# Where the token factors, the weight shares and the conversion's first step stand inside a group of a two-layer MLP

## The chip, the core and the metric

The kernel runs on one core of one Trainium2 chip. The core has five instruction streams that wait for each other through semaphores: TensorE (PE; its weight loads, PEld, overlap its matmuls), VectorE (DVE), ScalarE (ACT), GpSimd (POOL) and SyncE (SP), which here only starts DMAs. Each stream runs its instructions in the order in which they were written into it. The metric is the device time of one execution in microseconds (us). The kernel before takes 1313.79 us, the median of three runs (1312.47 to 1313.97).

## The reference

```python
# x: (2, 3008, 256); attention-like mixing along the sequence
X = np.fft.rfft(x, axis=1); Xr, Xi = X.real, X.imag
Yr = Xr @ w_r - Xi @ w_i + b_r
Yi = Xr @ w_i + Xi @ w_r + b_i
Yr, Yi = (np.sign(v) * np.maximum(np.abs(v) - 0.01, 0.0) for v in (Yr, Yi))
t = np.fft.irfft(Yr + 1j * Yi, n=3008, axis=1).reshape(6016, 256)
# two MLP layers, w_in: (256, 2048), w_out: (2048, 256)
h = t @ w_in1;  t = (h / (1 + np.exp(-1.702 * h))) @ w_out1
h = t @ w_in2;  t = (h / (1 + np.exp(-h))) @ w_out2
```

The four MLP weights arrive as float64 bit patterns (int64 arrays), and the kernel turns them into fp32 itself. Every matrix operand is split into a rounded part ("hi", made by ACT) and the rest ("lo", a subtraction on DVE or POOL), and each product is three matmuls: hi by hi, hi by lo, lo by hi.

## The kernel before, in words

**Stages.** The first 224 us hold a forward transform as matmuls, the mixing with its threshold ("mid"), and the inverse transform. Then comes the MLP. Its 6016 tokens are cut into six blocks: five of 1024 tokens and a last one of 896. A block is handled as two halves of n columns (n is 512, in the last block 448). For each of the two layers and each block there are eight **groups** p = 0 to 7, one for each pair of 128-wide chunks of the 2048 hidden features: 96 groups in all, written (layer, block, p). The function `group` is one of them.

**A group.** The four hidden quarters (two chunks by two halves) come out of seven products rather than eight, with seven **token factors** x0 to x6 (sums and differences of quarters of the block) and seven weight factors. `prod(X, 5, 4)` adds the product of weight factor 5 and token factor x4 to PSUM bank X; it is three matmuls. PE's order in a group is: x0, x1, six output matmuls, x2, x3, twelve output matmuls, x4, x6, six output matmuls, x5. That makes 21 matmuls on L774 and 24 on L746, 45 in all. The output matmuls (`out_next`) use the activations of the group before. Around them ACT copies and DVE adds: y1 is a copy of X (L796) plus Y (L798); y2 a copy of Z (L806) plus the later X (L815); y3 a copy of the same X (L808) plus the later Z (L819); y4 is taken from X directly. Each y goes through the activation (L777), a cast to hi (L779) and a subtraction for lo (L784; three on POOL, one on DVE). As X and Z are summed up in steps, PE may go on only when a step has been read: x3 after the copy L796, x4 after the copy L808, x6 after L806, x5 after the add L815, and the next group's x2 after the activation of y4. The y values lie in the columns of `yt` that held the block's own tokens.

**A border.** The last group of a block (p = 7) and the first of the next (p = 0) prepare the next block's token factors in `xprep`: a cast on ACT (L99), a subtraction on DVE (L100), and for two of them another on DVE that turns the temporary `tmp` into the next factor (L697, L699). x0 to x3 belong to p = 7, x4 to x6 to p = 0. `xsums`, in p = 6, makes two sums ahead of them.

**Weights inside the MLP.** A 128-by-256 unit of float64 is loaded (`cv_load`), ACT takes an absolute value (L155), DVE does five steps (L160 to L164, kept in the list `fill` and let out by `pump` and `fills`), and `settle` adds the two parts (L223). Block (0, 0) converts two units in each group, blocks (0, 1) to (0, 4) one, and the rest none. Units of the second layer are written to DRAM. In the last block of layer 0 and the first groups of layer 1, `fetch` brings them back and `moved` splits them into PE's operands: `place_in` with sums, four casts on ACT and eight DVE steps, `place_out` with a cast and a subtraction each.

**What sets the order.** `hook(h)` is called at six places in a group, and says what else is written there. The MLP from the second group on stands in regions that are kept in written order on all engines; the stages before and the first group are put in order by a scheduler's cost model (PE in the inverse stage, POOL and SP in the forward stage and SP in the mid stage are kept in written order there too). At the start of a region its first instructions can move ahead of the last ones of the region before. Which engine gets some steps is read from the table CFG, one letter for each call in turn (V is DVE, P is POOL).

Of the kernel before, what the change touches and what calls it, by code (L numbers as in the profile page):

```python
# [1047 lines left out]
```

## Time and profile before

| what | value |
|---|---|
| median of the three runs | 1313.79 us |
| the profiled execution's own time / its span | 1313.38 us / 1311.6 us |
| busy in the span: PE, PEld, DVE, ACT, POOL | 1217.0, 975.3, 723.2, 801.5, 545.3 us |
| PE idle in front of L774 / of L746 | 60.5 us / 2.2 us |
| chain that ended last, by engine | PE 50%, DVE 20%, ACT 16%, issue 5% |
| first stages (to 224 us): PE, DVE busy | 194.5, 205.9 us |
| mean granted TensorE clock | 0.973 |

Busy time is the sum of an engine's instructions. A line of the timeline is: start in us, duration, engine, source line, operation, output<-inputs, how many instructions were merged (x6), and in brackets how long the engine had been idle and what ended that. The granted clock is a share of full speed (2.4 GHz); 0.5 is 1.2 GHz.

### The profile page before, as it was taken

The numbers are of one execution on the slowest core, as the hardware profiler recorded it, in microseconds if no ns is written. First come the engines' busy times: TensorE is split into PE (matmuls) and PEld (weight loads), VectorE is DVE, ScalarE is ACT, GpSimd is POOL, SyncE is SP. The second block draws the span as 40 slices with busy tenths as digits, with TensorE's granted clock in tenths as the row PEclk, the third lists the DMA queues.
The fourth block names the chain that finished last, engine by engine and source line by source line (L and its number), as shares of the span: only waits on it lengthen the run. The fifth ranks groups of instructions, "written<-read, shape, count | busy, mean of one in ns | idle before, by whom it ended". The sixth has DMA issues, their size and how long they took to land.

```text
span 1311.6 us, 15384 instructions
## 1 busy us (share of the span) xinstructions
PE 1217.0 (93%) x5220; PEld 975.3 (74%) x5220; DVE 723.2 (55%) x1266; ACT 801.5 (61%) x1585; POOL 545.3 (42%) x472
## 2 busy tenths in 40 slices
PE   7899888798899899998999988999999999999998
PEld 4777677576687687786787866877868868778797
DVE  7899999767656555555555464243342332433422
ACT  3566644566565666656666766666666665665665
POOL 4665654454343434443443333333333333333333
PEclk9889979889899999999999989999999999999999
DMA  8441131111111110111110110000000000000000
GB/s 314 171 141 52 58 138 47 33 49 32 44 41 32 32 43 28 38 36 36 33 36 8 34 48 17 1 1 33 0 32 1 0 33 0 1 33 0 33 1 29
DMA packets 33010, 57.09 MB, mean 44 GB/s; under 512 B 3233, under 2 KB 22689, under 8 KB 31650
## 3 DMA queue, kind: packets, MB, share of 16 engines
q1 hardware_dynamic: 30882, 41.42, 9.9%
q0 software_dynamic: 2048, 14.68, 3.1%
q8 instruction: 41, 0.67, 0.2%
q14 instruction: 39, 0.32, 0.1%
...
## 4 chain that ended last, share of the span: by engine, by line
PE 50%; DVE 20%; ACT 16%; issue 5%; POOL 0%; DVEq 0%; ACTq 0%
PE o L746 25%; PE x L774 22%; ACT yt L777 6%; ACT g L779 4%; DVE x L100 3%; PE psi L358 2%; DVE yt L815 2%; ACT x L99 2%; ACT yt L796 2%; DVE yt L798 1%; DVE cv_c L160 1%; DVE cv_c L164 1%; DVE cv_a L162 1%; DVE th L521 1%; DVE f L537 1%
## 5 line engine op out<-in xcount | busy, mean ns | idle before, releaser
L784 POOL TENSOR_TENSOR g<-yt,g 128x512 fp32r<-128x512 f32 (+1 forms) x288 | 367.0, 1287 | 649.5 <-PE x L774 289.0
L774 PE MATMUL x<-x,wi 128*128 128x512 f32 (+1 forms) x2016 | 530.3, 400 | 60.5 <-DVE yt L815 24.8
L746 PE MATMUL o<-g,wo 128*128 128x512 f32 (+1 forms) x2304 | 582.2, 395 | 2.2 <-POOL g L784 1.3
L746 PEld LDWEIGHTS o<-g,wo 128*128 128x128 f32 x2304 | 438.6, 191 | 101.2 <-POOL g L784 3.1
L774 PEld LDWEIGHTS x<-x,wi 128*128 128x128 f32 x2016 | 378.0, 191 | 170.2 <-DVE yt L815 27.6
L777 ACT ACTIVATE yt<-yt 128x512 f32<-128x512 f32 (+1 forms) x288 | 179.1, 622 | 346.6 <-DVE yt L815 252.4
L779 ACT CAST g<-yt 128x512 fp32r<-128x512 f32 (+1 forms) x384 | 234.2, 611 | 12.0
L798 DVE TENSOR_TENSOR yt<-yt,x 128x512 f32<-128x512 f32 (+1 forms) x96 | 64.9, 676 | 184.1 <-ACT yt L796 175.8
L815 DVE TENSOR_TENSOR yt<-yt,x 128x512 f32<-128x512 f32 (+1 forms) x96 | 64.6, 673 | 166.7 <-PE x L774 166.0
L784 DVE TENSOR_TENSOR g<-yt,g 128x512 fp32r<-128x512 f32 (+1 forms) x96 | 65.3, 681 | 63.5 <-ACT g L779 63.5
L100 DVE TENSOR_TENSOR x<-yt,x 128x512 fp32r<-128x512 f32 (+1 forms) x48 | 47.0, 980 | 59.9 <-ACT x L99 59.4
L160 DVE TENSOR_SCALAR cv_c<-cv_c 128x256 f32<-128x256 f32 x64 | 45.9, 718 | 44.0 <-ACT cv_c L155 44.0
L819 DVE TENSOR_TENSOR yt<-yt,x 128x512 f32<-128x512 f32 (+1 forms) x96 | 64.6, 673 | 0.6
L806 ACT COPY yt<-x 128x512 f32<-128x512 f32 (+1 forms) x96 | 54.5, 568 | 13.8 <-DVE x L100 13.8
L796 ACT COPY yt<-x 128x512 f32<-128x512 f32 (+1 forms) x96 | 54.9, 571 | 3.3 <-PE x L774 3.2
L777 ACT ACTIVATE yt<-x 128x512 f32<-128x512 f32 (+1 forms) x96 | 56.2, 585 | 0.2 <-PE x L774 0.2
L808 ACT COPY yt<-x 128x512 f32<-128x512 f32 (+1 forms) x96 | 55.7, 580 | 0.6 <-PE x L774 0.6
L358 PE MATMUL psi<-m,fh 128*128 128x376 f32 (+3 forms) x208 | 52.3, 341 | 0.2 <-DVE sd L511 0.2
L223 POOL TENSOR_TENSOR cv_a<-cv_a,cv_c 128x256 f32<-128x256 f32 x48 | 41.0, 857 | 9.9 <-DVE cv_c L164 9.9
L498 PE MATMUL psm<-wc_hi,xtl 128*128 128x512 f32 x96 | 38.0, 399 | 5.1 <-DVE xtl L100 5.1
L358 PE MATMUL psf<-m,xh 128*128 128x376 f32 (+1 forms) x160 | 39.5, 343 | 2.5 <-ACT xh L309 1.5
L358 PE MATMUL psi<-m,fl 128*128 128x376 f32 (+3 forms) x104 | 36.0, 346 | 6.2 <-POOL fl L100 3.3
(121 smaller groups left out, 1098.2 us busy)
## 6 DMA issues: line engine op xcount, KB each, us to landing
...
```

The costliest lines, as they stand in the source:

```text
L100: (lo_eng or nc.vector).tensor_sub(lo, src, r32(hi))
L160: lambda: ts(c, c, C_HI, None, op0=ALU.min),
L358: nc.tensor.matmul(ps, a, z, start=i == 0 and x == 0, stop=i == last and x == 2)
L746: nc.tensor.matmul(acc[h, mm], st, mv, start=first and k == 0, stop=last and k == 2)
L774: nc.tensor.matmul(ps, st, mv, start=first and m == 0, stop=m == 2, skip_group_check=True)
L777: nc.scalar.activation(g, g if src is None else src, func)
L779: nc.scalar.copy(gh, g)
L784: eng.tensor_sub(gl, g, r32(gh))
L796: nc.scalar.copy(y1, X)
L798: nc.vector.tensor_add(y1, y1, Y)
L815: nc.vector.tensor_add(y2, y2, X)
L819: nc.vector.tensor_add(y3, y3, Z)
```

## The change

Five things, all in the written order:

1. The token factors. `xprep` can be called in two parts (cast, subtraction). In p = 7, x0 goes from hook 2 to hook 1 (ahead of y1's activation), x1 and x2 from hook 3 to hook 2 (ahead of the copies of y2 and y3), x3's cast goes from hook 4 to hook 3 (ahead of y2's activation instead of behind it), and its subtraction stays at hook 4, which itself is moved behind the adds of y2 and y3. In p = 0, x4 goes to hook 1 and x6 to hook 2; x5 stays at hook 3. `xsums` goes to hook 1.
2. The absolute values (L155) go from hook 2 to hook 1, ahead of y1's activation; in blocks without conversions all fill steps are let out at once behind hook 2.
3. The fetched weights: `fetch` is written one group ahead, `place_in` goes from hook 3 to hook 2 and all its subtractions to DVE, `place_out`'s subtractions all go to POOL.
4. In CFG, `cva` goes from 'PPVP' to 'P' and `pil` from 'PPVV' to 'P': all L223 adds and all subtractions of freshly converted input weights go to POOL. The spare quarter of `yt` is no longer their temporary; `tmp` is.
5. The storage of y2 and y3 is exchanged, so that y2 overwrites the quarter that x1 and the last `tmp` step read, and y3 the one that x4 reads.

```diff
-    def xprep(l, i, k):
+    def xprep(l, i, k, part=3):
...
-        hi, lo = (slot(0, F32R, "x")[:, :n] for _ in range(2))
-        split(hi, lo, src, lo_eng=E('xl1' if l else 'xl0' if i == 0 else 'xl', k))
-        xb[l, i, k] = (hi, lo)
-        if k == 2:
-            nc.vector.tensor_sub(xtmp[0], b22, xtmp[0])
-        if k == 3:
-            nc.vector.tensor_sub(xtmp[0], b21, xtmp[0])
+        if part & 1:
+            xb[l, i, k] = tuple(slot(0, F32R, "x")[:, :n] for _ in range(2))
+            nc.scalar.copy(xb[l, i, k][0], src)
+        if part & 2:
+            hi, lo = xb[l, i, k]
+            E('xl1' if l else 'xl0' if i == 0 else 'xl', k).tensor_sub(lo, src, r32(hi))
+            if k in (2, 3):
+                nc.vector.tensor_sub(xtmp[0], b22 if k == 2 else b21, xtmp[0])
...
-        (y1, y2), (y3, y4) = y
-        spare[:] = [y4]
+        (y1, y3), (y2, y4) = y
...
-        fills(2)
+        fills(1 if l or i == last else 2)
...
-        hook(4)
         prod(Z, 6, 6, False)
         nc.vector.tensor_add(y3, y3, Z)
         rest(nc.vector, *g22)
         g12 = gate(0, 1, y3)
         rest(nc.gpsimd, *g12)
+        hook(4)
...
-                    place_in(l, c + r, a, E('mvl', r), sums_c)
+                    place_in(l, c + r, a, nc.vector, sums_c)
                 else:
-                    place_out(l, c + r, a, E('mvl', r))
+                    place_out(l, c + r, a, nc.gpsimd)
...
-            for x in {2: (0,), 3: (1, 2), 4: (3,)}.get(h, ()) if more else ():
-                xprep(*nxt, x)
-            for x in {2: (4,), 3: (6, 5)}.get(h, ()) if p == 0 else ():
-                xprep(l, i, x)
-            if h == 2 and p == NPR - 2 and (l, i) != (1, last):
+            if more:
+                if h in (1, 2):
+                    for x in ((0,), (1, 2))[h - 1]:
+                        xprep(*nxt, x)
+                if h == 3:
+                    xprep(*nxt, 3, 1)
+                if h == 4:
+                    xprep(*nxt, 3, 2)
+            if p == 0 and h < 4:
+                xprep(l, i, {1: 4, 2: 6, 3: 5}[h])
+            if h == 1 and p == NPR - 2 and (l, i) != (1, last):
                 xsums(*nxt)
-            if h == (3 if len(done) < 3 else 2):
+            if h == (3 if len(done) < 3 else 1):
                 window(0, done)
                 done[:] = []
-            if h == 2:
+            if h == 1:
                 window(k, ())
-            if h == 3:
-                moved(fetched)
+            if h in (2, 3):
+                moved([f for f in fetched if (f[0][0] == "in") == (h == 2)])
             if h == 5:
+                fetched[:] = fetch_for(at + 1)
+            if h == 4:
                 pump()
```

**Place 1, DVE at the border from block (0, 2) to (0, 3).** Before, from y1's add in p = 7 (L798) to the same add in the next group; L815 and L819 are the adds of y2 and y3, L784 an activation's lo, and x and tmp are the token factors and their temporary:

```order
L798 TENSOR_TENSOR yt<-yt,x 128x512
L100 TENSOR_TENSOR x<-yt,x 128x512
...
L100 TENSOR_TENSOR x<-yt,x 128x512
L100 TENSOR_TENSOR x<-tmp,x 128x512
L697 TENSOR_TENSOR tmp<-yt,tmp 128x512
L163 TENSOR_SCALAR cv_c<-cv_a 128x256
...
L815 TENSOR_TENSOR yt<-yt,x 128x512
L100 TENSOR_TENSOR x<-tmp,x 128x512
L699 TENSOR_TENSOR tmp<-yt,tmp 128x512
L819 TENSOR_TENSOR yt<-yt,x 128x512
L784 TENSOR_TENSOR g<-yt,g 128x512
L798 TENSOR_TENSOR yt<-yt,x 128x512
```

The same stretch of the changed kernel, where the four adds and the lo are L800, L817, L820, L800 and L786, and the token factors L699 and L701:

```order
L800 TENSOR_TENSOR yt<-yt,x 128x512
L699 TENSOR_TENSOR x<-yt,x 128x512 x2
L699 TENSOR_TENSOR x<-tmp,x 128x512
L701 TENSOR_TENSOR tmp<-yt,tmp 128x512
L160 TENSOR_SCALAR cv_c<-cv_c 128x256
...
L817 TENSOR_TENSOR yt<-yt,x 128x512
L820 TENSOR_TENSOR yt<-yt,x 128x512
L786 TENSOR_TENSOR g<-yt,g 128x512
L699 TENSOR_TENSOR x<-tmp,x 128x512
L701 TENSOR_TENSOR tmp<-yt,tmp 128x512
L800 TENSOR_TENSOR yt<-yt,x 128x512
```

x3's subtraction and the `tmp` step behind it have gone from between the adds of y2 and y3 to behind y2's lo; the fill steps have gone behind x0, x1 and x2.

**Place 2, ACT at the same border.** Before, from the copy of y1 in p = 7 to the activation of y2 (L777 the activations, L779 the casts to hi, L99 the casts of token factors, L155 the absolute value):

```order
L796 COPY yt<-x 128x512
L777 ACTIVATE yt<-yt 128x512
L779 CAST g<-yt 128x512
L99 CAST x<-yt 128x512
L155 ACTIVATE cv_c<-raw_4547 128x256
L806 COPY yt<-x 128x512
L808 COPY yt<-x 128x512
L99 CAST x<-yt 128x512
L99 CAST x<-tmp 128x512
L777 ACTIVATE yt<-yt 128x512
```

The same in the changed kernel (L798, L808 and L810 are the copies, L779 and L781 the activation and its cast, L696 the token factors):

```order
L798 COPY yt<-x 128x512
L696 CAST x<-yt 128x512
L155 ACTIVATE cv_c<-raw_4545 128x256
L779 ACTIVATE yt<-yt 128x512
L781 CAST g<-yt 128x512
L696 CAST x<-yt 128x512
L696 CAST x<-tmp 128x512
L808 COPY yt<-x 128x512
L810 COPY yt<-x 128x512
L696 CAST x<-tmp 128x512
L779 ACTIVATE yt<-yt 128x512
```

x0's cast and the absolute value now stand ahead of y1's activation, and the casts of x1 and x2 ahead of the copies of y2 and y3.

**Place 3, ACT in the second group of the last block of layer 0**, where input weights (wi) that were fetched (cv_ld) and their sums (cv_s) are split. Before:

```order
L779 CAST g<-yt 128x448
L806 COPY yt<-x 128x448
L808 COPY yt<-x 128x448
L99 CAST wi_6328<-cv_ld 128x256
L99 CAST wi_6328<-cv_ld 128x128
L99 CAST wi_6328<-cv_s 128x256 x2
L777 ACTIVATE yt<-yt 128x448
```

Changed:

```order
L781 CAST g<-yt 128x448
L99 CAST wi_6324<-cv_ld 128x256
L99 CAST wi_6324<-cv_ld 128x128
L99 CAST wi_6324<-cv_s 128x256 x2
L808 COPY yt<-x 128x448
L810 COPY yt<-x 128x448
L779 ACTIVATE yt<-yt 128x448
```

The four casts have gone ahead of the copies of y2 and y3.

## Rows read from the trace of the kernel before

**Rows 1.** Busy time by stretch: its start and end in us, its length, then busy us and instructions of PE, PEld, DVE, ACT and POOL, the granted clock, the DMA share and GB/s. The first two are the stages before the MLP and block (0, 0); the third is a group in the middle of block (0, 2), the fourth one in the last block of layer 1.

```profile
0.00:224.04 224.04, 194.45 (x912) 160.98 (x912) 205.90 (x399) 117.53 (x305) 126.50 (x121) 0.93 0.39 135
224.04:326.11 102.07, 85.22 (x313) 64.02 (x314) 70.50 (x134) 61.95 (x129) 53.17 (x52) 0.90 0.13 37
472.20:482.70 10.50, 10.50 (x47) 8.44 (x46) 5.74 (x10) 6.56 (x13) 4.55 (x5) 1.00 0.12 45
...
1250.07:1259.31 9.24, 9.24 (x47) 8.45 (x46) 2.49 (x4) 5.65 (x12) 3.43 (x4) 1.00 0.00 0
```

**Rows 2.** The same view, of stretches that begin with the copy of y1 (L796) in p = 7 of a block and end with that of a later group: blocks (0, 0) to (0, 1), five groups; (0, 2) to (0, 3), four groups; (0, 4) to (0, 5), four; (0, 5) to (1, 0), three; (1, 0) to (1, 1), three; (1, 2) to (1, 3), three; (1, 4) to (1, 5), three.

```profile
320.74:381.70 60.96, 56.81 (x223) 42.54 (x222) 36.74 (x62) 38.55 (x73) 25.27 (x23) 0.94 0.12 37
503.70:552.18 48.48, 45.21 (x182) 34.38 (x181) 27.73 (x48) 31.06 (x58) 17.74 (x16) 0.96 0.12 33
684.68:727.31 42.63, 40.74 (x186) 34.12 (x185) 22.09 (x43) 30.27 (x63) 14.66 (x13) 1.00 0.02 7
...
770.09:811.60 41.51, 34.14 (x132) 27.24 (x131) 22.73 (x42) 28.55 (x59) 13.73 (x13) 0.88 0.09 26
864.17:898.78 34.61, 32.55 (x137) 24.96 (x136) 16.09 (x23) 23.52 (x43) 11.94 (x10) 1.00 0.08 31
1039.61:1075.45 35.84, 32.59 (x137) 24.96 (x136) 16.52 (x23) 23.52 (x43) 11.56 (x10) 1.00 0.08 30
1216.29:1248.83 32.54, 30.64 (x138) 25.15 (x137) 15.12 (x23) 21.97 (x43) 11.22 (x10) 1.00 0.09 33
```

**Rows 3.** Timeline of the border from (0, 2) to (0, 3), p = 7 and then p = 0 from 518.75 us on.

```profile
504.31 0.69 DVE L798 TENSOR_TENSOR yt<-yt,x 128x512 f32<-128x512 f32 x1 [2.06 <-ACT yt L796]
506.45 1.30 POOL L784 TENSOR_TENSOR g<-yt,g 128x512 fp32r<-128x512 f32 x1 [0.42 <-PE x L774]
506.87 1.43 DVE L100 TENSOR_TENSOR x<-yt,x 128x512 fp32r<-128x512 f32 x1 [1.87 <-ACT x L99]
508.98 1.33 PE L774 MATMUL x<-x,wi 128*128 128x512 f32 x5
509.21 0.68 DVE L100 TENSOR_TENSOR x<-yt,x 128x512 fp32r<-128x512 f32 x1
511.81 0.68 DVE L815 TENSOR_TENSOR yt<-yt,x 128x512 f32<-128x512 f32 x1
512.54 2.37 PE L774 MATMUL x<-x,wi 128*128 128x512 f32 x9 [0.60 <-DVE yt L815]
515.70 0.68 DVE L819 TENSOR_TENSOR yt<-yt,x 128x512 f32<-128x512 f32 x1
516.41 0.63 ACT L777 ACTIVATE yt<-yt 128x512 f32<-128x512 f32 x1 [2.08 <-DVE yt L819]
518.75 0.58 ACT L796 COPY yt<-x 128x512 f32<-128x512 f32 x1
519.38 1.13 PE L774 MATMUL x<-x,wi 128*128 128x512 f32 x2 [1.91 <-ACT yt L796]
520.73 3.95 PE L746 MATMUL o<-g,wo 128*128 128x512 f32 x12
523.41 0.59 ACT L806 COPY yt<-x 128x512 f32<-128x512 f32 x1 [1.18 <-DVE x L100]
528.33 1.87 PE L774 MATMUL x<-x,wi 128*128 128x512 f32 x7 [0.41 <-DVE yt L815]
```

**Rows 4.** Timeline of the border from (1, 2) to (1, 3), and of the add and the copy that follow it two groups later.

```profile
1046.21 0.68 DVE L815 TENSOR_TENSOR yt<-yt,x 128x512 f32<-128x512 f32 x1
1050.10 0.68 DVE L819 TENSOR_TENSOR yt<-yt,x 128x512 f32<-128x512 f32 x1
1053.78 0.97 PE L774 MATMUL x<-x,wi 128*128 128x512 f32 x3 [1.73 <-ACT yt L796]
...
1071.20 0.69 DVE L815 TENSOR_TENSOR yt<-yt,x 128x512 f32<-128x512 f32 x1 [3.91 <-PE x L774]
1075.45 0.58 ACT L796 COPY yt<-x 128x512 f32<-128x512 f32 x1
```

**Rows 5.** Two stretches of block (0, 5), as in rows 1 (a group that splits input weights alone, and one that splits output weights too).

```profile
718.01:727.31 9.30, 9.30 (x46) 8.30 (x45) 4.81 (x12) 6.97 (x17) 3.45 (x4) 1.00 0.00 0
727.31:737.99 10.68, 9.58 (x47) 8.29 (x46) 5.24 (x13) 7.58 (x19) 4.14 (x5) 1.00 0.17 50
```

**Rows 6.** Timeline of the second of these groups, and of PE in p = 7 of the same block.

```profile
731.72 0.80 SPq L250 DMA_DIRECT2D cv_ld<-w_out  x2
732.95 0.81 ACT L99 CAST wi<-cv_s 128x256 fp32r<-128x256 f32 x2 [1.27 <-DVE cv_s L198]
734.80 2.12 PE L774 MATMUL x<-x,wi 128*128 128x448 f32 x9 [1.10 <-DVE yt L815]
...
780.02 4.05 PE L774 MATMUL x<-x,wi 128*128 128x448 f32 x9 [3.37 <-DVE yt L815]
```

**Rows 7.** Groups of instructions by line in the first 224 us, POOL and then DVE: busy us, mean ns of one, idle time ahead of them.

```profile
L223 POOL TENSOR_TENSOR cv_a<-cv_a,cv_c 128x256 f32<-128x256 f32 x15 | 13.4, 893 | 9.9 <-DVE cv_c L164 9.9
...
L223 DVE TENSOR_TENSOR cv_a<-cv_a,cv_c 128x256 f32<-128x256 f32 x5 | 4.6, 911 | 0.1
L100 DVE TENSOR_TENSOR wi<-cv_a,wi 128x256 fp32r<-128x256 f32 (+1 forms) x4 | 2.9, 734 | 0.6 <-ACT wi L99 0.6
```

**Rows 8.** Timeline of PE in block (0, 0), waiting behind the ten fill steps.

```profile
277.08 3.32 PE L774 MATMUL x<-x,wi 128*128 128x512 f32 x7 [1.92 <-DVE yt L815]
```

More of the change, by code (lines that the diff above doesn't have):

```diff
@@ L10 @@
 F32 = mybir.dt.float32
-CFG = {'lv0': 'V', 'lv': 'VVVVVPVVVVVP', 'dd0': 'VPVVPPPPPVVP', 'dd': 'VVVVVVVVVVPV', 'mpl': 'VPPVVP', 'ths': 'VVVVPV', 'thf': 'PVPVVPVV', 'fsl': 'VPVVVVPV', 'ivf': 'PVVPVVVVVPPVPPVV', 'cva': 'PPVP', 'pol': 'PPPP', 'pil': 'PPVV', 'mvl': 'PVVP', 'xl': 'V', 'xse': 'V', 'gl': 'VPPPPPPP', 'tf': [6, 9, 12], 'tm': [2, 3, 4, 5, 7, 14], 'ti': [2, 2, 3, 4, 5, 10, 12, 13, 13, 15], 'kb': [2, 2, 2, 2, 2, 2, 2, 2], 'kr': 1, 'fa': 3, 'fe': 2, 'xp': [2, 4, 4, 5], 'xq': [1, 4, 1], 'xs': 4, 'xi': [11, 12, 13, 15], 'xsi': 9, 'ca': 4, 'tl': True, 'fwd': 'Pool,SP', 'rest0': 'all', 'rest1': 'all', 'last1': 'all', 'inv': 'PE', 'mid': 'SP', 'last0': 'all', 'thm': 'A', 'gl0': 'PVPVVVPV', 'gl2': 'PPPPPPPP', 'gl3': 'PPPPPPPV', 'xl0': 'V', 'xl1': 'V', 'pre': 17, 'pre2': 0, 'yd': 6, 'nf': 4, 'lvb': 6, 'mlp': 'none', 'pr': 'VVVP', 'pf': 'PV', 'eo': '0000', 'ddb': 6, 'mlp1': 'all', 'mlp2': 'all'}
+CFG = {'lv0': 'V', 'lv': 'VVVVVPVVVVVP', 'dd0': 'VPVVPPPPPVVP', 'dd': 'VVVVVVVVVVPV', 'mpl': 'VPPVVP', 'ths': 'VVVVPV', 'thf': 'PVPVVPVV', 'fsl': 'VPVVVVPV', 'ivf': 'PVVPVVVVVPPVPPVV', 'cva': 'P', 'pol': 'PPPP', 'pil': 'P', 'mvl': 'PVVP', 'xl': 'V', 'xse': 'V', 'gl': 'VPPPPPPP', 'tf': [6, 9, 12], 'tm': [2, 3, 4, 5, 7, 14], 'ti': [2, 2, 3, 4, 5, 10, 12, 13, 13, 15], 'kb': [2, 2, 2, 2, 2, 2, 2, 2], 'kr': 1, 'fa': 3, 'fe': 2, 'xp': [2, 4, 4, 5], 'xq': [1, 4, 1], 'xs': 4, 'xi': [11, 12, 13, 15], 'xsi': 9, 'ca': 4, 'tl': True, 'fwd': 'Pool,SP', 'rest0': 'all', 'rest1': 'all', 'last1': 'all', 'inv': 'PE', 'mid': 'SP', 'last0': 'all', 'thm': 'A', 'gl0': 'PVPVVVPV', 'gl2': 'PPPPPPPP', 'gl3': 'PPPPPPPV', 'xl0': 'V', 'xl1': 'V', 'pre': 17, 'pre2': 0, 'yd': 6, 'nf': 4, 'lvb': 6, 'mlp': 'none', 'pr': 'VVVP', 'pf': 'PV', 'eo': '0000', 'ddb': 6, 'mlp1': 'all', 'mlp2': 'all'}
 NUM = dict(tf=[5, 9, 13], tm=[1, 3, 5, 7, 9, 11], ti=[0, 2, 4, 6, 8, 10, 12, 14, 14, 15, 15], kb=[2] * 8, kr=1, fa=3, fe=2, pm=0, nf=4, lvb=6, ddb=8, ivb=1, eob=2, fsb=6, f1=3, f2=0, fm=[7, 8, 9], fi=[1, 1, 2, 2], pre=13, pre2=1, yd=3, psh=0, ie=[12], xp=[1, 3, 4, 5], xq=[1, 2, 2], xs=5, nw=4, xi=[14, 14, 15, 15], xsi=13, rw=2, ca=4, cc=2, tb=1, tmn=1)
@@ L853, in rate, with fetch_for @@
         return 0 if l == 1 or i == last else N('kb')[p] if i == 0 else N('kr')
+    def fetch_for(at):
+        units = moves.get(seq[at], ()) if at < len(seq) else ()
+        return [(u, [fetch(u[0], u[1], u[2] + r) for r in range(2)]) for u in units]
+    fetched = fetch_for(0)
     done = settle()
```

1 line of the change is left out of this document (removed).

## The prediction

> **What bounds the kernel now.** I read the busy time by stretch first. In the middle of a block a group takes 10.50 us, and PE is busy in all of them; in the last block, with 448 columns, it takes 9.24 [rows 1]. That is 45 matmuls of 0.233 or 0.205 us, so there nothing but fewer matmuls helps, and an engine that is made earlier gains nothing. What a change of order can win lies elsewhere: at the borders between blocks, in block (0, 0) (PE busy 85.22 of 102.07 us at a granted clock of 0.90) and in the first 224 us, where DVE is busy 205.90 us.
>
> The stretches over borders give what each costs above PE's own time [rows 2]: (0, 0) to (0, 1) 60.96 - 5 x 10.5 = 8.5; (0, 2) to (0, 3) 48.48 - 42 = 6.5, which I use for three borders; (0, 4) to (0, 5) 42.63 - 10.5 - 3 x 9.24 = 4.4; (0, 5) to (1, 0) 41.51 - 9.24 - 21 = 11.3; (1, 0) to (1, 1) 3.1; (1, 2) to (1, 3) 35.84 - 31.5 = 4.3, used for three; (1, 4) to (1, 5) 3.6. The sum is 63.3 us.
>
> Then the timeline of one border [rows 3] says which wait ends last. In p = 7 the add of y2 comes at 511.81, and PE waits 0.60 for it. The add of y3 comes only at 515.70, since DVE first does x3's lo, which waits for a cast that ACT runs behind y2's activation, and the tmp step. Everything on ACT behind y3 is late by that much: the copy of y1 of the next group is at 518.75, and PE, which needs it before x3, waits 1.91. Undisturbed, the way from y2's add to that copy is 1075.45 - 1071.20 = 4.25 us [rows 4]; here it is 6.94. In p = 0 the copy of y2 waits 1.18 more for x4's lo, whose source it overwrites. After the 1.91 the granted clock is at 1.2 GHz for a stretch: twelve matmuls take 3.95 us rather than 2.8. In layer 1 the same gap stands between 1046.21 and 1050.10, with a wait of 1.73.
>
> **The change part by part.**
>
> *x3 behind y3 (4 x 512 columns of DVE and ACT work moved, none removed).* The 6.94 becomes 4.25: 2.7 us off the path at every border. What is late next is y2's add itself. DVE does the same list before it, three lo's, a tmp step and five fill steps, in another order. Today the first lo starts at 506.87, takes 1.43 instead of 0.68 (row at 509.21) and ends 0.55 after POOL's lo of 506.45 to 507.75; the rest takes until 511.81, 3.5 us. In the new order x0's lo is done before that POOL instruction (its cast stands right behind the copy at 503.70), x1's meets it instead and ends at the same 508.3, and so one lo less (0.6) remains: y2's add at 511.2, ended at 511.9. PE wants it at 508.98 + 12 x 0.233 = 511.8. So no wait worth counting, and the next copy of y1 comes at 511.2 + 4.25 = 515.45 instead of 518.75.
>
> *p = 0.* From the copy of y1 to x5 it takes 528.33 - 518.75 = 9.58 us now. x4's cast stands ahead of y1's activation in the new order, its source is overwritten by y3 rather than y2, and the 1.18 goes: 515.45 + 8.4 = 523.85. PE's own time says 511.9 + 10.5 = 522.4, and part of the 1.15 lost to the clock goes too; I leave 1.2 us of loss per border. Three borders of layer 0: 3 x (6.5 - 1.2) = 15.9. At (0, 0) to (0, 1) ten fill steps stand before y2's add instead of five, which costs 8.5 - 6.5 = 2.0 now; with one POOL instruction of 1.3 more I leave 1.2 + 2.0 + 1.3 = 4.5: 4.0. At (0, 4) to (0, 5) there are no fill steps: 4.4 - 0.6 = 3.8. Layer 1 has none either, and the walk above finds y2's add ready before PE asks; I leave 0.3 at each of five borders: 3.1 + 13.0 + 3.6 - 1.5 = 18.2.
>
> *place_in ahead of the copies.* This costs. In block (0, 5) a group that splits input weights alone runs at PE's rate today, 9.30, one that splits output weights too takes 10.68 [rows 5]. In the new order PE's x4 waits for the copy of y3, which stands behind four casts, two of them behind DVE's sums. I count from the copy of y1: DVE's lo of the first cast is held by POOL's lo (at 506.45, 2.75 us behind the copy in rows 3) until about 4.0; sums and last cast 5.0, copies done 6.0, x4 and the add of y2 0.9 more, and 3.8 to the next copy (the 4.25, for 448 columns): 10.7 us. Today ACT waits 1.27 for the same sums with the copies already done [rows 6], under twelve output matmuls, which end at about 4. So two groups lose 1.4 each, those at 10.68 stay, and xsums ahead of the sums costs (0, 5, 6) another 0.6: -3.3. In (0, 5, 7) and (1, 0, 0) token factors and weights pile up before the copies; the 3.37 us wait of today [rows 6] becomes one of about 4.5 at x4, while the 2.7 of x3 goes. I get 13.6 + 14.7 + 9.4 = 37.7 us against 41.51: +3.8. Below zero it could be 5 us worse, at best all 11.3 goes.
>
> *Fetching a group ahead.* The DMA for output weights goes out at 731.72, right when its buffer is free and a group before its use [rows 6]; SP has nothing else to wait for. So writing it earlier changes nothing: 0. Its cover is SP's empty queue.
>
> *The conversion.* Where PE sets the pace, the absolute value ahead of y1's activation falls into ACT's idle time before it and gains nothing. In block (0, 0) ten fill steps hold y2's add and PE waits, as 1.92 us at 277.08 [rows 8]; they can start earlier in six groups by the gap that DVE has behind y1's add (1.87 us at 506.87 [rows 3]), but then run beside POOL's adds. Between nothing and 6 x 1.9 = 11, I take 3, as the 1.43 of rows 3 shows that DVE steps beside POOL stand still.
>
> *CFG.* In the first 224 us DVE loses five adds (4.6 us) and eight lo's (2.9 for four) and POOL gets thirteen instructions of about 0.89 us [rows 7]. If DVE's time is the path, up to 10 us are won; if POOL holds DVE each time, up to 13 x 0.89 - 10 = 2 lost, with a slip in the order of the scheduler on top. I take 0. POOL itself has room: it is busy 4.55 of 10.50 us in a group [rows 1].
>
> The row at 506.87 shows a DVE instruction with two SBUF inputs that ends only after POOL's. The Trainium skill says the same in "SBUF — State Buffer", section "Who interferes with whom": a Vector instruction with two SBUF inputs and a GpSimd instruction that reads SBUF share one pair of ports, held for a whole instruction, and the later one stands still. By that rule moving adds and lo's from DVE to POOL saves DVE little, and a longer POOL instruction blocks it instead: the 0 would be a small loss, and the first rival below would be nearer.
>
> Sum: 15.9 + 4.0 + 3.8 + 18.2 - 3.3 + 3.8 + 3.0 = 45.4 us. The profiled execution took 1313.38 us, 0.4 below the median of the runs, so 1313.8 - 45.4 = 1268.4, and I say 1268.
>
> **The rivals.**
>
> *POOL holds DVE more often.* The new order brings x0 and x4 beside POOL's last lo's and adds of the group before. If each border meets two more POOL instructions of 1.3 us, eleven borders give back 11 x 2.6 = 28 and block (0, 0) its 3, less what PE's lead hides: 1294. For it: the 1.43 of rows 3. Against: POOL is idle more than half of a group.
>
> *DVE's relief counts.* If in the first 224 us up to 10 are won and block (0, 0) loses its waits (102.07 - 85.22 = 17 us, and 1.2 GHz for part of it), some 18 more come: 1250. For it: DVE is busy 92% there. Against: the same POOL.
>
> *Slower: the copies of y2 and y3 behind the casts.* If in p = 7 the casts of x1 and x2 make the copy of y3 come after PE's twelve output matmuls, the wait moves from x3 to x4 and the borders gain nothing; in block (0, 5) and (1, 0, 0) eight groups pay 2.7 us for four casts each, and the time is 1313 + 22 = 1335. It decides from the point where the copy ends after 508.98. Y1's activation can start at 505.0, when the add of 504.31 is done, and five steps of 0.585 us (516.41 to 518.75 are four) and the copy's 0.58 later it is 508.5: a lead of 0.5. A later y1 activation by that much brings a part of it, but all of it takes 6 us.
>
> *Nothing changes,* because another wait of the same length stands behind each that goes: 1313. PE's idle time at the borders speaks against it.
>
> **How the numbers follow.** The forecast has 0.68, its own range 1256 to 1282 (the border terms by 8 either way, block (0, 5) and the first stages by 5 each). POOL holding DVE has 0.15, DVE's relief 0.11, slower 0.03, no change 0.03. A range of 1250 to 1290 takes in the forecast and about half of each neighbour: 0.8. Faster by over 0.2% (about what a measurement of this kernel tells from no change): 0.94; within it 0.03; slower 0.03.
>
> **What would show it.** Right: the stretches of p = 7 and p = 0 in layer 1 at 10.5 us each, in layer 0 within 1.2 of it together; no DVE instruction between the adds of y2 and y3; no 1.2 GHz at the border at 519; groups of block (0, 5) all near 10.7 with PE waiting for the copy of y3. Wrong: PE waiting at x4 in borders without weights; token factors of 1.4 us beside POOL more than once a border; the MLP starting more than 5 us off 224.

## The result, and the profile after

The changed kernel takes 1284.01 us, the median of three runs (1280.16 to 1284.30). The ratio to the kernel before is 0.9767, with an interval of 0.9737 to 0.9797: 30 us less, where 45 were forecast. The range of 1250 to 1290 holds it; the forecast's own narrower range, 1256 to 1282, misses it by 2 us. Five more runs of it, in another series, have a median of 1284.63 (1281.38 to 1285.54) and a ratio of 0.9748 (0.9728 to 0.9769). The profiled execution is the quickest of the first three: 1280.16, with a span of 1278.4, 33.2 less than before.

The first view is the busy time by stretch, as in [rows 1, 2]: start and end, length, then busy us of PE, PEld, DVE, ACT and POOL, the granted clock, the DMA share and GB/s. The stretches begin and end with the copy of y1 of the same groups as there: first stages, block (0, 0), (0, 0) to (0, 1), (0, 2) to (0, 3), one group of block (0, 5), (0, 5) to (1, 0), (1, 0) to (1, 1), (1, 2) to (1, 3), (1, 4) to (1, 5).

```profile
0.00:227.74 227.74, 193.82 (x912) 159.10 (x912) 207.92 (x385) 118.21 (x305) 138.61 (x135) 0.93 0.38 133
227.74:323.65 95.91, 81.64 (x313) 61.84 (x313) 70.06 (x119) 62.26 (x130) 64.09 (x66) 0.93 0.14 39
318.45:377.43 58.98, 55.48 (x223) 43.14 (x222) 39.15 (x61) 38.26 (x73) 26.95 (x25) 0.94 0.13 38
495.29:539.66 44.37, 42.98 (x182) 33.48 (x181) 30.79 (x47) 30.91 (x59) 19.73 (x17) 1.00 0.11 36
711.52:722.29 10.77, 9.50 (x47) 8.36 (x46) 5.78 (x12) 7.57 (x19) 4.87 (x6) 1.00 0.16 49
755.09:795.81 40.72, 33.98 (x136) 28.18 (x135) 21.99 (x39) 28.90 (x58) 15.84 (x16) 0.87 0.09 26
848.31:880.65 32.34, 32.10 (x137) 25.10 (x136) 16.52 (x23) 23.20 (x43) 12.26 (x10) 1.00 0.09 33
1017.15:1048.65 31.50, 31.50 (x137) 25.34 (x136) 18.54 (x23) 23.52 (x43) 12.04 (x10) 1.00 0.09 34
1185.12:1215.58 30.46, 30.23 (x137) 25.25 (x136) 15.68 (x23) 21.65 (x43) 11.45 (x10) 1.00 0.10 35
```

Three readings. A border in the middle of layer 1 is at PE's own rate: 31.50 of 31.50. The same border in layer 0 is not: 44.37 against 42. And the first stages are longer by 3.7 us, with 14 DVE instructions fewer (385 for 399) but 2 us more of DVE's time. The table sets the profiled executions against each other, boundary by boundary (copies of y1); its last column adds up to 33.2.

| stretch | forecast gain | measured gain |
|---|---|---|
| first stages, to 224.04 / 227.74 | 0 | -3.7 |
| block (0, 0), up to p = 7 | 3.0 | 6.0 |
| (0, 0) to (0, 1) | 4.0 | 2.0 |
| three borders of layer 0 | 15.9 | 12.4 |
| (0, 4) to (0, 5) | 3.8 | 2.1 |
| groups of block (0, 5) | -3.3 | -3.8 |
| (0, 5) to (1, 0) | 3.8 | 0.8 |
| five borders of layer 1 | 18.2 | 17.4 |

The waits of PE by releaser (us in all, how often, the longest) say what is late now. L810 is the copy of y3, L817 the add of y2, L798 the copy of y1:

```profile
PE x L776 <- ACT yt L810: 15.6, 8, 3.6
PE x L776 <- DVE yt L817: 14.1, 9, 3.4
...
PE x L776 <- ACT yt L798: 2.6, 3, 2.2
```

The wait for y1's copy, which the change was forecast to take away, has shrunk to three: 2.17 at the start of the MLP and 0.23 at each of the two borders into a block of 448 columns. None is left at the other borders. The timeline of the border (0, 2) to (0, 3) [rows 3], here p = 7 from 495.29 and p = 0 from 507.16 on, shows how:

```profile
495.29 0.58 ACT L798 COPY yt<-x 128x512 f32<-128x512 f32 x1
496.51 0.96 DVE L699 TENSOR_TENSOR x<-yt,x 128x512 fp32r<-128x512 f32 x1
498.04 1.31 POOL L786 TENSOR_TENSOR g<-yt,g 128x512 fp32r<-128x512 f32 x1
498.46 1.43 DVE L699 TENSOR_TENSOR x<-yt,x 128x512 fp32r<-128x512 f32 x1 [0.99 <-ACT x L696]
499.34 0.58 ACT L810 COPY yt<-x 128x512 f32<-128x512 f32 x1
500.57 1.56 PE L776 MATMUL x<-x,wi 128*128 128x512 f32 x6
502.57 0.42 DVE L164 SCALAR_TENSOR_TENSOR cv_c<-raw,cv_c 128x256 f32<-128x256 uint32 x1
502.92 0.68 DVE L817 TENSOR_TENSOR yt<-yt,x 128x512 f32<-128x512 f32 x1
503.52 0.68 DVE L820 TENSOR_TENSOR yt<-yt,x 128x512 f32<-128x512 f32 x1
506.35 1.74 DVE L701 TENSOR_TENSOR tmp<-yt,tmp 128x512 f32<-128x512 f32 x1
507.16 0.58 ACT L798 COPY yt<-x 128x512 f32<-128x512 f32 x1
510.56 1.64 DVE L699 TENSOR_TENSOR x<-yt,x 128x512 fp32r<-128x512 f32 x1 [0.77 <-ACT x L696]
514.97 0.68 DVE L817 TENSOR_TENSOR yt<-yt,x 128x512 f32<-128x512 f32 x1
515.80 2.34 PE L776 MATMUL x<-x,wi 128*128 128x512 f32 x9 [1.18 <-DVE yt L817]
```

The add of y3 now follows that of y2 at once (503.52 behind 502.92), and the next copy of y1 comes 507.16 - 502.92 = 4.24 us behind y2's add, where it took 6.94. But y2's add itself still comes 7.63 us behind y1's copy, right behind a fill step, and in p = 0 it comes 7.81 behind and PE waits 1.18 for it. The granted clock of the whole stretch is 1.00, and the 1.2 GHz behind the wait of 1.91 in [rows 3] is gone. It was no part of what the border cost, though. The other two borders of layer 0 before the change, (0, 1) to (0, 2) and (0, 3) to (0, 4), have the same wait, 1.91 and 1.92, and their four groups take as long as the 48.48 of [rows 2] at a granted clock of 1.00:

```profile
413.20:461.70 48.50, 43.81 (x182) 33.26 (x181) 27.73 (x48) 31.05 (x58) 17.76 (x16) 1.00 0.11 33
594.18:642.68 48.50, 43.83 (x182) 33.25 (x181) 27.74 (x48) 31.04 (x58) 17.76 (x16) 1.00 0.11 33
```

### The profile page after: what moved, and what is told of

Read it like the earlier page. It is cut to its first block, busy times and chain, and to the rows that moved or that the text cites. A ratio compares the mean times of both kernels' runs of the same rounds, so it can differ in the third digit from the quotient of the medians.

```text
span 1278.4 us, 15403 instructions
## 1 busy us (share of the span) xinstructions
PE 1202.4 (94%) x5220; PEld 973.4 (76%) x5220; DVE 751.9 (59%) x1222; ACT 801.0 (63%) x1585; POOL 587.3 (46%) x516
## 4 chain that ended last, share of the span: by engine, by line
PE 55%; ACT 9%; DVE 7%; issue 3%; DVEq 0%; ACTq 0%
PE o L748 29%; PE x L776 26%; ACT yt L779 3%; ACT g L781 2%; DVE yt L817 1%; DVE x L699 1%; ACT yt L798 1%; ACT x L696 1%; DVE yt L800 1%; DVE wi L100 1%; ACT yt L808 0%; DVE cv_c L160 0%; DVE cv_a L162 0%; ACT wi L99 0%; ACT yt L810 0%
## 5 line engine op out<-in xcount | busy, mean ns | idle before, releaser
L786 POOL TENSOR_TENSOR g<-yt,g 128x512 fp32r<-128x512 f32 (+1 forms) x288 | 372.5, 1305 | 567.7 <-DVE g L786 301.2
L776 PE MATMUL x<-x,wi 128*128 128x512 f32 (+1 forms) x2016 | 518.6, 396 | 36.6 <-ACT yt L810 15.6
L779 ACT ACTIVATE yt<-yt 128x512 f32<-128x512 f32 (+1 forms) x288 | 179.0, 622 | 295.2 <-DVE yt L817 248.3
L781 ACT CAST g<-yt 128x512 fp32r<-128x512 f32 (+1 forms) x384 | 234.1, 611 | 11.7
L817 DVE TENSOR_TENSOR yt<-yt,x 128x512 f32<-128x512 f32 (+1 forms) x96 | 64.8, 675 | 210.4 <-PE x L776 210.2
L800 DVE TENSOR_TENSOR yt<-yt,x 128x512 f32<-128x512 f32 (+1 forms) x96 | 64.9, 676 | 174.5 <-ACT yt L798 173.5
L786 DVE TENSOR_TENSOR g<-yt,g 128x512 fp32r<-128x512 f32 (+1 forms) x96 | 66.1, 688 | 66.5 <-ACT g L781 66.4
L699 DVE TENSOR_TENSOR x<-yt,x 128x512 fp32r<-128x512 f32 (+1 forms) x48 | 54.3, 1132 | 28.7 <-ACT x L696 28.7
L223 POOL TENSOR_TENSOR cv_a<-cv_a,cv_c 128x256 f32<-128x256 f32 x64 | 62.9, 988 | 15.7 <-DVE cv_c L164 15.6
L820 DVE TENSOR_TENSOR yt<-yt,x 128x512 f32<-128x512 f32 (+1 forms) x96 | 64.9, 676 | 2.2 <-PE x L776 1.1
L779 ACT ACTIVATE yt<-x 128x512 f32<-128x512 f32 (+1 forms) x96 | 56.2, 585 | 3.9 <-PE x L776 3.9
L810 ACT COPY yt<-x 128x512 f32<-128x512 f32 (+1 forms) x96 | 55.7, 580 | 1.0 <-PE x L776 1.0
L798 ACT COPY yt<-x 128x512 f32<-128x512 f32 (+1 forms) x96 | 54.8, 571 | 1.8 <-PE x L776 1.8
L808 ACT COPY yt<-x 128x512 f32<-128x512 f32 (+1 forms) x96 | 54.9, 571 | 0.0
L358 PE MATMUL psi<-m,fh 128*128 128x376 f32 (+3 forms) x208 | 48.9, 324 | 3.0 <-ACT fh L99 1.7
L163 DVE TENSOR_SCALAR cv_c<-cv_a 128x256 uint32<-128x256 uint32 x64 | 43.3, 678 | 1.4
L155 ACT ACTIVATE cv_c<-raw 128x256 f32<-128x256 f32 x64 | 27.4, 438 | 22.9 <-DMA raw<-in_wi 19.8
```

What stands on the lines that cost most here:

```text
L223: E('cva', u[2]).tensor_add(a, a, c)
L358: nc.tensor.matmul(ps, a, z, start=i == 0 and x == 0, stop=i == last and x == 2)
L699: E('xl1' if l else 'xl0' if i == 0 else 'xl', k).tensor_sub(lo, src, r32(hi))
L776: nc.tensor.matmul(ps, st, mv, start=first and m == 0, stop=m == 2, skip_group_check=True)
L779: nc.scalar.activation(g, g if src is None else src, func)
L781: nc.scalar.copy(gh, g)
```

## The experiments

Each was timed beside the kernel before, in its own series; ratios are to that. The medians of the kernel before lie between 1313.79 and 1317.22 in these series, so a difference of two or three us between medians of two series is not certain by itself. In the diffs "-" is the kernel named as the base.

**Order of the token factors alone.** Kernel before with parts 1 and 5 of the change (`xprep` in two parts, the hooks of x0 to x6 and `xsums`, the storage of y2 and y3); conversion, weights and CFG as before.

> The kernel before with only the token factors' new order and the exchanged storage of y2 and y3 (parts 1 and 5 of the change); the conversion, the fetched weights and CFG as before. Theory (the gain is x3 leaving the gap between the adds of y2 and y3): the borders inside layer 1 cost 0 as in the changed kernel, those inside layer 0 about 2, block (0, 5) stays at 9.3 and 10.7 us per group, the MLP starts at 224: 1276 to 1282 us, no slower than the whole change. Rival (the parts need each other: the absolute values ahead of y1's activation and all lo's on POOL are what brings DVE forward): borders in layer 0 still cost 4 or more, 1290 to 1300 us.

Measured: 1276.25 us (1275.66 to 1279.17), ratio 0.9707 (0.9681 to 0.9733). The order of the factors gives more than the whole change does. What is left of the change costs some 8 us by the medians (5 by the ratio 0.9748 of the second series), and not the nothing that my other terms add up to (-3.3 + 3.0 + 0).

**CFG back.** Base: the changed kernel.

```diff
-'cva': 'P', 'pol': 'PPPP', 'pil': 'P'
+'cva': 'PPVP', 'pol': 'PPPP', 'pil': 'PPVV'
```

> The changed kernel with cva and pil back at PPVP and PPVV. Theory (POOL's adds hold DVE, so moving them bought nothing): the MLP starts near 224 again instead of 227.7, borders of layer 0 that have their add on DVE lose the 1.2 us wait; in all 2 to 6 us faster than the changed kernel, 1276 to 1281. Rival (DVE's relief carries block (0, 0)): the stretch of block (0, 0) goes from 84 back to 90 us, 1286 to 1290.

Measured: 1280.35 (1279.00 to 1281.06), ratio 0.9729 (0.9709 to 0.9750): 3.7 less than the changed kernel, within the theory's range. By itself this is weak, since the intervals of the two ratios overlap and the two profiled executions are equally long (1278.4). The MLP starts at 226.3, not near 224, and PE's wait for y2's add at the borders of layer 0 is still 1.19 to 1.20: that part of the theory failed. The run on CFG alone, below, is the clearer one.

**place_in behind the copies again.** Base: the changed kernel.

```diff
-            if h in (2, 3):
-                moved([f for f in fetched if (f[0][0] == "in") == (h == 2)])
+            if h == 3:
+                moved(fetched)
```

> The changed kernel with place_in back at hook 3, behind the copies of y2 and y3; its subtractions stay on DVE, place_out's on POOL. Theory: groups (0, 5, 1) and (0, 5, 2) at 9.3 instead of 10.8 us, (0, 5, 3) to (0, 5, 6) at 9.3 to 10.7, p = 7 and (1, 0, 0) shorter by 1 each: 4 to 9 us faster than the changed kernel, 1274 to 1279. Rival (the casts only move the wait back to y2's add): block (0, 5) unchanged, 1281 to 1285.

Measured: 1276.81 (1276.37 to 1277.16), ratio 0.9704 (0.9684 to 0.9723): 7.2 less. In block (0, 5) of the changed kernel the timeline reads:

```profile
713.80 0.60 ACT L99 CAST wi<-cv_ld 128x256 fp32r<-128x256 f32 x2
715.70 0.81 ACT L99 CAST wi<-cv_s 128x256 fp32r<-128x256 f32 x2 [1.30 <-DVE cv_s L198]
716.42 0.53 ACT L808 COPY yt<-x 128x448 f32<-128x448 f32 x1
716.84 0.54 ACT L810 COPY yt<-x 128x448 f32<-128x448 f32 x1
717.43 1.50 PE L776 MATMUL x<-x,wi 128*128 128x448 f32 x6 [1.27 <-ACT yt L810]
```

ACT waits 1.30 for DVE's sums in the middle of the casts, and the copies stand behind that. With the casts behind the copies a group that splits input weights alone is at PE's rate again, and one that splits output weights too takes 10.49 for 10.77, by the stretches of this run:

```profile
692.45:701.75 9.30, 9.08 (x44) 7.93 (x43) 4.66 (x12) 6.97 (x17) 3.13 (x3) 1.00 0.10 30
711.24:721.73 10.49, 9.58 (x46) 8.29 (x45) 5.38 (x12) 7.58 (x18) 5.03 (x6) 1.00 0.17 51
```

The groups p = 1 to 7 of block (0, 5) are 4.9 us shorter together, the first two of (1, 0) 1.4.

**Absolute values back.** Base: the changed kernel; `window` at hook 2 again, which takes the placing of freshly converted weights along.

> The changed kernel with the absolute values (and the placing of freshly converted weights) back at hook 2, behind y1's activation. Theory (the gap on DVE behind y1's add is where block (0, 0) gained its 6 us): its six groups lose 1 us each, 1287 to 1291; the borders stay as they are. Rival (block (0, 0) is held by POOL, not by the fill steps' start): no change, 1281 to 1285.

Measured: 1285.13 (1284.64 to 1289.27), ratio 0.9774 (0.9749 to 0.9799): not told apart from the changed kernel in time, and nearer the rival's range than the theory's. Its trace does show block (0, 0) longer, 100.5 us against 95.9 (and 95.5 in a second profile of the changed kernel). So this part gains some 4.6 us there, where the theory says 6, and the time shows one at most. The start of the MLP differs between executions by nearly as much (228.0 here, 227.7 and 231.2 in the two profiles of the changed kernel), so the time alone can't settle this one.

**Both back.** Base: the changed kernel, with CFG as before and `place_in` behind the copies.

> Changed kernel with CFG as before (cva PPVP, pil PPVV) and place_in behind the copies again. Theory that the parts add by stage: the order of the token factors alone gave 1276.25; the absolute values ahead of y1's activation shorten block (0, 0) by some 6 us (102.1 to 95.9 between its first copies of y1), and nothing else is lost: 1269 to 1273, with the MLP starting within 2.5 us of 224. Rival, that the later start of the MLP in the changed kernel (227.7) has nothing to do with CFG: the MLP still starts at 227 or later and the time is 1274 to 1277.

Measured: 1273.79 (1271.56 to 1275.05), ratio 0.9683 (0.9656 to 0.9710). The parts add up as the first theory has it, 0.8 above its upper end; the MLP starts at 226.4, and block (0, 0) takes 97.1.

**x3 alone.** Base: the kernel before.

```diff
-            for x in {2: (0,), 3: (1, 2), 4: (3,)}.get(h, ()) if more else ():
+            for x in {2: (0,), 3: (1, 2)}.get(h, ()) if more else ():
                 xprep(*nxt, x)
+            if more and h in (3, 4):
+                xprep(*nxt, 3, h - 2)
...
-        hook(4)
         prod(Z, 6, 6, False)
...
         rest(nc.gpsimd, *g12)
+        hook(4)
```

> Kernel before with one thing changed: x3's cast stands ahead of y2's activation and its subtraction and the tmp step behind the adds of y2 and y3. Theory of the prediction, that this stretch between the two adds (6.94 us against 4.25) was what PE waited for: 2.5 us at each of eleven borders, 1284 to 1290, and the 1.2 GHz stretch at the border near 519 goes. Rival, that the lo's and tmp step ahead of y2's add hold it as long, so that x3 alone gives less than half: 1300 or more.

Measured: 1291.74 (1291.17 to 1295.86), ratio 0.9832 (0.9805 to 0.9858): 22.8 us. That is 1.7 us slower than the theory's range and 8 us faster than the rival's. At a border of layer 1, p = 7 falls from 13.5 to 10.8, and what is late next stands in the timeline of p = 0 (its copy of y1 is at 1034.80). L699 here is x4's lo, L808 and L810 the copies of y2 and y3:

```profile
1038.19 1.42 DVE L699 TENSOR_TENSOR x<-yt,x 128x512 fp32r<-128x512 f32 x1 [1.87 <-ACT x L696]
1039.69 0.58 ACT L808 COPY yt<-x 128x512 f32<-128x512 f32 x1 [1.53 <-DVE x L699]
...
1040.82 1.98 PE L776 MATMUL x<-x,wi 128*128 128x512 f32 x6 [0.91 <-ACT yt L810]
```

**x3, and the order of p = 0.** Base: x3 alone.

```diff
-            for x in {2: (4,), 3: (6, 5)}.get(h, ()) if p == 0 else ():
+            for x in {1: (4,), 2: (6,), 3: (5,)}.get(h, ()) if p == 0 else ():
```

> As e7_x3_alone (1291.74), and in p = 0 x4 stands at hook 1, x6 at hook 2 and x5 at hook 3, as in the changed kernel; p = 7 keeps x0, x1 and x2 at their old hooks and the storage is not exchanged. Theory that x4's place alone frees the copies of y2 and y3 in p = 0: the group of p = 0 falls from 13.05 to 10.9 in layer 1 and from 13.7 to 12.5 in layer 0, 1275 to 1279. Rival, that x0's earlier place in p = 7 does it through the copy of y1: 1286 or more.

Measured: 1278.18 (1277.01 to 1279.22), ratio 0.9716 (0.9695 to 0.9737): 13.6 less than with x3 alone. The groups p = 0 take 10.8 in layer 1 and 12.5 in layer 0, as the theory says. The border (1, 2) to (1, 3), and with it the wait above, is done with; its stretch reads:

```profile
1015.77:1047.27 31.50, 31.50 (x137) 25.34 (x136) 17.99 (x23) 23.50 (x43) 12.06 (x10) 1.00 0.09 34
```

So x3 behind y3 and the earlier hooks of x4 and x6 hold 36.7 of the 38.6 us of the factor order (1314.92 - 1278.18 and 1314.88 - 1276.25, each with the median of before in its series). What x0, x1 and x2 in p = 7 and the exchange of storage bring beyond that, some two, isn't told apart from nothing. The edit moves x6 with x4: the row of 1039.69 above puts the wait on x4's lo, but x4 was not tried without x6.

**No exchange of storage.** Base: the factor order alone.

```diff
-        (y1, y3), (y2, y4) = y
+        (y1, y2), (y3, y4) = y
```

> Factor order alone (1276.25) without the exchange of y2's and y3's storage, so that y2 overwrites x4's source. Theory of the prediction, that the 1.18 us for which the copy of y2 waited for x4's lo is what the exchange takes away: about 1.2 us at each of ten borders, 1286 to 1290. Rival, that x4's lo, now a hook earlier, is done before the copy of y2 in any case: 1275 to 1278.

Measured: 1276.78 (1276.49 to 1276.96), ratio 0.9711 (0.9689 to 0.9732). Rival right: where x4 stands a hook earlier, it does not matter which of y2 and y3 overwrites its source.

**CFG alone, on the factor order.** Base: the factor order alone, with `cva` and `pil` both 'P'.

> Factor order alone (1276.25) with the two letters of CFG (cva P, pil P) in addition. Theory that POOL's added instructions hold DVE in the first stages, where DVE is busy nearly all the time: the MLP starts 2 to 4 us later than 224.5, at 227 or more, and the time is 1278 to 1281. Rival, DVE's relief or nothing: the MLP starts at 222 to 225.5 and the time is 1274 to 1277.

Measured: 1282.13 (1277.62 to 1283.04), ratio 0.9728 (0.9706 to 0.9751) against 0.9707 (0.9681 to 0.9733). The intervals overlap; the start of the MLP is the clean sign: 229.4 against 224.5, five us later and more than the 2 to 4 that the theory says. First stretches and lines of the first stages without the two letters (lines: busy us and mean ns of one, then idle time ahead):

```profile
0.00:224.45 224.45, 195.03 (x912) 161.13 (x912) 203.75 (x399) 118.00 (x304) 127.62 (x121) 0.93 0.39 135
```

```profile
L162 DVE SCALAR_TENSOR_TENSOR cv_a<-raw,cv_c 128x256 uint32<-128x256 uint32 x20 | 9.1, 469 | 0.0
L100 DVE TENSOR_TENSOR xtl<-xt,xth 128x512 fp32r<-128x512 f32 x12 | 8.6, 726 | 1.2 <-ACT xth L99 1.2
...
L161 DVE TENSOR_SCALAR cv_c<-cv_c 128x256 uint32<-128x256 uint32 x20 | 5.9, 310 | 0.0
```

and with them:

```profile
0.00:229.42 229.42, 194.79 (x912) 161.34 (x912) 207.64 (x386) 118.18 (x305) 137.15 (x134) 0.93 0.39 132
```

```profile
L162 DVE SCALAR_TENSOR_TENSOR cv_a<-raw,cv_c 128x256 uint32<-128x256 uint32 x20 | 12.7, 645 | 0.0
...
L100 DVE TENSOR_TENSOR xtl<-xt,xth 128x512 fp32r<-128x512 f32 x12 | 11.4, 957 | 3.5 <-ACT xth L99 3.5
L161 DVE TENSOR_SCALAR cv_c<-cv_c 128x256 uint32<-128x256 uint32 x20 | 9.1, 463 | 0.1
```

The adds L223 on POOL, in the same view without and with the letters:

```profile
L223 POOL TENSOR_TENSOR cv_a<-cv_a,cv_c 128x256 f32<-128x256 f32 x15 | 13.2, 879 | 11.4 <-DVE cv_c L164 11.4
```

```profile
L223 POOL TENSOR_TENSOR cv_a<-cv_a,cv_c 128x256 f32<-128x256 f32 x20 | 22.7, 1139 | 16.1 <-DVE cv_c L164 16.1
```

Thirteen instructions go from DVE to POOL, and DVE's busy time grows by 3.9 us, because the ones that stay take longer: L161 463 ns for 310, L162 645 for 469. Over fourteen profiles (two of before and after, twelve of these runs) the MLP starts between 223.8 and 226.4 us in the nine without the two letters, and between 227.7 and 231.2 in the five with them; the means are 4.5 apart.

**Fill steps behind y3.** Base: both back.

```diff
-        fills(1 if l or i == last else 2)
+        late = l == 0 and 0 < i < last and p == 0
+        if not late:
+            fills(1 if l or i == last else 2)
...
-        fills(1)
+        if not late and (l, i) != (0, 0):
+            fills(1)
```

> As e5_both_back, and in p = 0 of blocks (0, 1) to (0, 4) the five fill steps stand behind the add of y3, in block (0, 0) the second five of ten do. Theory that fill steps ahead of y2's add are what is left at these borders: PE's wait of 1.18 for y2's add in p = 0 goes, about 1.2 us at each of four borders, and block (0, 0) loses 3 to 6 us more of its waits: 6 to 10 us below e5_both_back. Rival, that DVE's work is only moved and the next y1's add or the next weights come later by as much: within 2 us of e5_both_back.

Measured: 1280.22 (1279.45 to 1282.97), ratio 0.9741 (0.9717 to 0.9765): 6.4 slower than its base, worse than either expected. In p = 0 of layer 0 the wait for y2's add went, and the group takes 10.9 for 12.5; but p = 1 takes 10.9 for 9.5, so that a border gains 0.2 us in all (44.2 for 44.4). The timeline from p = 0 to p = 1, where L812 is the copy of y3:

```profile
523.03 2.87 POOL L786 TENSOR_TENSOR g<-yt,g 128x512 fp32r<-128x512 f32 x2 [4.98 <-DVE cv_c L161]
523.46 1.28 DVE L163 TENSOR_SCALAR cv_c<-cv_a 128x256 uint32<-128x256 uint32 x1
524.77 1.40 DVE L164 SCALAR_TENSOR_TENSOR cv_c<-raw,cv_c 128x256 f32<-128x256 uint32 x1
527.03 0.68 DVE L800 TENSOR_TENSOR yt<-yt,x 128x512 f32<-128x512 f32 x1
530.05 1.67 PE L776 MATMUL x<-x,wi 128*128 128x512 f32 x6 [0.85 <-ACT yt L812]
```

Behind y3 the fill steps meet POOL's two lo's, take 1.28 and 1.40 instead of 0.29 and 0.42, and push y1's add of the next group back. What makes the kernel slower is block (0, 0): 105.6 us for 97.1, with a PE wait of 10.05 in p = 2 for a copy of y3.

**No conversion at the borders.** Base: both back.

```diff
-        return 0 if l == 1 or i == last else N('kb')[p] if i == 0 else N('kr')
+        if l == 0 and 0 < i < last:
+            return (0, 1, 2, 1, 2, 1, 1, 0)[p]
+        return 0 if l == 1 or i == last else N('kb')[p]
```

> As e5_both_back, but in blocks (0, 1) to (0, 4) no unit is converted in p = 7 and p = 0, and two in p = 2 and p = 4. Theory that the five fill steps ahead of y2's add are all that is left at these borders (2.4 us each): the groups of p = 7 and p = 0 come down to 10.5 to 11 each, 7 to 9 us less than e5_both_back, 1264 to 1267. Rival, that ten fill steps in one group hold y2's add as they do in block (0, 0): p = 2 and p = 4 take 1 to 2 us more each, and the time is 1271 to 1275.

Measured: 1261.97 (1261.33 to 1264.96), ratio 0.9586 (0.9567 to 0.9606), below what the theory says. The border (0, 2) to (0, 3), four groups as above, is at PE's rate:

```profile
487.51:529.52 42.01, 42.01 (x182) 33.81 (x181) 29.03 (x43) 30.76 (x58) 17.00 (x14) 1.00 0.10 32
```

The five fill steps have gone from p = 7 and p = 0, and the unit's absolute value and POOL's add with them. A token factor's lo still meets POOL's there and takes 1.42 for 0.68:

```profile
490.69 1.42 DVE L699 TENSOR_TENSOR x<-yt,x 128x512 fp32r<-128x512 f32 x1 [0.99 <-ACT x L696]
```

The groups with ten fill steps lose nothing either: p = 2 takes 10.50, p = 4 takes 10.69, and p = 5 gives that back with 10.31. Blocks (0, 1) to (0, 4) are 11.3 us shorter than with both back (339.5 for 350.8); block (0, 1) alone gives 5.6 of it. This is the fastest of all, 1.8% below the changed kernel by the medians of the same series (1261.97 and 1284.63).

## Why the prediction came out as it did

The wait that ends last at a border was named rightly, and most parts were priced too high. Between the two profiled executions 33.2 of the 45.4 us came: of the eight rows of the table above one, block (0, 0), brought more than its forecast and the other seven less. That the wide range holds the result is owed to its margin, which the forecast's own range did not have.

**Right: which wait ends last at a border.** x3 between the adds of y2 and y3 was what PE waited for. Alone it gives 22.8 us, the walk from y2's add to y1's copy is 4.24 where I took 4.25, and 17.4 of the 18.2 forecast for layer 1 came. The 1.2 GHz near 519, which I read as a cost of the border, cost nothing: two borders without it were as long.

**Right in part of its cause: p = 0.** I put the end of the 1.18 down to two things, x4's cast being earlier and its source being overwritten by y3. The exchange does nothing beside the earlier hook (1276.78 without it, 1276.25 with it); the earlier hooks of x4 and x6 do it, and they are worth 13.6 us, since without them the wait moves on to PE at x4, 0.91.

**Mis-sized: three borders of layer 0, 15.9, measured 12.4.** The step that failed is "so no wait worth counting". I placed y2's add 7.5 us behind y1's copy in p = 7; it comes 7.63 behind. The 0.1 isn't the fault: in a group at PE's rate the add must come 10.5 - 4.25 = 6.25 behind, or the next copy of y1 is late, whether PE waits at x5 or not. p = 7 takes 11.87 for this reason with no wait of PE worth a line, p = 0 another two us, and p = 1 gives one back; 2.4 is left where I left 1.2. That the conversion's unit in these two groups is what is left was shown by taking it out of both: then nothing is left. That its fill steps hold y2's add in p = 0 was shown by moving them behind it, which took PE's wait away there. At (0, 0) to (0, 1) 2.0 came for 4.0, and 0.7 in the second profile of the changed kernel (60.23 us for 60.96); whether that is the same error stays open.

**Mis-sized: borders into the 448-column block.** For (0, 4) to (0, 5) I took 42.63 less 10.5 and three times 9.24 as lost. The row itself says PE busy 40.74 at a granted clock of 1.00 [rows 2]: only 1.9 was idle there, so 3.8 could not come. It gave 2.1, and (1, 4) to (1, 5) gave 2.1 of the 3.6 I had read in the same way. By shape, the trace of before has 63 matmuls of 512 columns in that stretch, output matmuls of the block before among them, and 123 of 448: 63 x 0.233 + 123 x 0.205 = 39.9 us, where I had taken 38.2.

**Right, and the wrong trade: place_in.** 10.7 us for each group of block (0, 5) was forecast, 10.77 measured, with PE at x4 behind the copy of y3. The loss was taken as -3.3 there and +3.8 at (0, 5) to (1, 0). There I had let the 11.3 above PE's own time shrink to 7.5, since the wait of x3 goes; but the copies are held in those groups too, with waits of 3.61 and 3.13 for L810, and only 0.8 came. Undone, the part gives 7.2 us back.

**Wrong sign: CFG, forecast 0.** Its bounds were 10 won to 2 lost, and it lost 3.7 by the median of CFG back; two other pairs of kernels that differ in it give 5.9 (1282.13 and 1276.25) and 3.0 (1276.81 and 1273.79). All are beyond the lower bound. The failed step is "2 lost": I priced POOL holding DVE as thirteen instructions of 0.89 less the DVE time that goes. But the DVE time that goes was not won, since the steps that stay take longer, and L223 on POOL is no 0.89 any more: 1.14 in the mean of twenty, against 0.88 of fifteen. The sentence in the prediction on the shared pair, from the Trainium skill, "SBUF — State Buffer", section "Who interferes with whom", gave the right sign, and the trace agrees: thirteen fewer instructions on DVE and 3.9 us more of its time. I had left it out of the sum, and that sum's 0 leant to the winning side.

**Under-sized: block (0, 0), 3.0, measured 6.0.** The bound of 11 stood; the absolute values ahead of y1's activation bring 4.6 (100.5 to 95.9, by the run in which only they and the placing of fresh weights stand otherwise). The group that falls most is p = 1, which takes 8.35 for 12.0, but that is not their doing in the main: with them alone back it takes 9.22, and p = 2 takes 25.35 for 23.52. POOL holds the fill steps there too; that this is why not all of the 11 came is not shown. In the timeline of the changed kernel the same step is first beside POOL's lo and then, for the second unit, alone:

```profile
269.85 1.48 POOL L786 TENSOR_TENSOR g<-yt,g 128x512 fp32r<-128x512 f32 x1
270.20 1.28 DVE L163 TENSOR_SCALAR cv_c<-cv_a 128x256 uint32<-128x256 uint32 x1
...
274.50 0.29 DVE L163 TENSOR_SCALAR cv_c<-cv_a 128x256 uint32<-128x256 uint32 x1
```

**The rivals.** That POOL holds DVE is what the first stages show. At the borders it came as the rival says, and as the prediction's own sign of being wrong has it: at (0, 2) to (0, 3) two DVE instructions were held before (1.43 and 1.41 us), and five are now (0.96, 1.43, 1.74, 1.19 and 1.64, where each takes 0.67 to 0.69 alone). In p = 7 that is 1.0 us ahead of y2's add. It doesn't decide alone, since in layer 1, and without the conversion in layer 0, such borders run at PE's rate; what share it has in the 2.4 left in layer 0 was not tried. That copies stand behind casts, the slower rival, is what happens in block (0, 5) and (1, 0), with 1.27 a group; at the borders its condition was not met: y3's copy is done at 499.92, and PE comes to x4 behind it at 500.57, without a wait. Fetching a group ahead was not tried by itself, nor were the two letters of CFG apart.

**What stays open.** Why the profiled start of the MLP varies by two to three us between kernels that agree in CFG; and whether the absolute values cost some of this there.
